# Opening of a transformer block on one core: one tile's statistics on ScalarE, scalings by halves, keys' exponentials later

## The chip, the cores and the metric

The kernel runs on one core of one Trainium2 chip. The metric is the device time of one execution in microseconds (us), from one launch. Five engines work beside each other, each through its own queue in order: TensorE (PE in the profile, with its weight loads as PEld), VectorE (DVE), ScalarE (ACT), GpSimd (POOL) and SyncE (SP), which here issues the DMAs. They wait for one another through semaphores.

## What is computed

The reference is a transformer block in fp32 with adaptive layer norms, over 2048 tokens of width 1024. Cut to what matters here:

```python
mod = silu(c) @ w_mod                       # six vectors of 1024
sa, ca, ga, sb, cb, gb = mod
h = layernorm(x) * (1 + ca) + sa            # over each token's 1024 values
x = x + ga * A(h)                           # attention with a memory, below
h = layernorm(x) * (1 + cb) + sb
x = x + gb * ((gelu(h @ w_gate) * (h @ w_up)) @ w_down)

def A(h):                                   # 32 heads of 32, 4 segments of 512 tokens
    for s in range(4):                      # qs, ks, vs: segment s of h @ wq, h @ wk, h @ wv
        a_dot = softmax(qs @ ks.T * scale + causal) @ vs
        a_mem = (phi(qs) @ M) / (phi(qs) @ z + 1e-6)
        o = g * a_mem + (1 - g) * a_dot     # g = sigmoid(beta)
        M += phi(ks).T @ vs ; z += phi(ks).sum()
    return concat(o) @ wo                   # phi(t) = t + 1 where t > 0, else exp(t)
```

The layer norm divides by the root of the variance plus 1e-5.

## The kernel before, in words

Activations are held transposed, as eight feature tiles of 128 features by 512 tokens for each segment. Matmuls get nearly fp32 accuracy from operands split in a high and a low part (`hi`, `lo`), and three products: high by high, low by high, high by low. The attention goes through 32 steps of four heads and one segment each; behind it come the output projection and the feed-forward part.

The change lies in the opening (`opening`, L1850), which prepares the first two segments and the first two steps. Every engine's order is written out by hand there: the string `OPENING` (L1845) is read word by word, each word emits some instructions, and each engine executes what it gets in that order.

For the second segment the words do the following.

- `x0` to `x3` load its four tiles of 128 tokens (`x1_load`, each 512 KB, named `rx` in the trace, L127). The loads go into four buffers that other raw data leave earlier.
- `t0` to `t3` take the statistics of a tile (`stats`, L1901): on VectorE two `bn_stats` of 512 columns (L227), their aggregate (L230), the variance plus eps (L232) and the negated mean (L1904); on POOL the power -0.5 (L233) and the product of mean and power (L1905).
- `b0` to `b3` normalize a tile in place (`scaled`, L1908), in two halves of 512 features: tile 0 on ScalarE (L1915), tiles 1 to 3 on VectorE (L1913).
- Each `N` is a piece of `norm_seg` (L332): the first makes the four transposes of feature tile 0 on PE (L341, tile `tpa`), and each later one reads a turned feature tile on ScalarE (`h`, L348), splits it in high and low parts (`hha`, L352 or L354; `hla`, L356 or L359), and transposes the next feature tile. Feature tiles 0 to 3 need the first halves of all four token tiles, 4 to 7 the second halves. Five `N` stand in the opening; the rest of them are called from the first step of the attention.
- Each `F` is a piece of `first_part` (L568) for the first segment: eight times the projections of one feature tile (L583, L586), then the keys' copies (`kn`, L415), then the values' copies (`vx`, L417), then the list `AFTER[0]`: `qo` splits the queries (`qh` L462, `ql` L466), `dq` copies them by DMA (L422), `kt` transposes the keys (L433) and splits them (`kh` L436, `kl` L437), `dk` copies them, `ek` takes the keys' exponentials (L444 on ScalarE, L445 and L447 on VectorE), and `ea` and `eb` do nothing in the first segment.
- `V` makes ten matmuls whose results nobody reads (L1944, `full`), which keep PE at work while it waits. `S` changes the pool of PSUM tiles. `g` works out the shares from beta on VectorE.

The projections of the second segment follow from the first attention step, by another `first_part`, again L583 and L586. Behind five of their eight feature tiles come the first scores (L615).

Of the kernel before, what the change touches and what calls it, by code (L numbers as in the profile page):

```python
# [13 lines left out]
AF = mybir.ActivationFunctionType  # L14
ALU = mybir.AluOpType
# [4 lines left out]
P = 128  # L20
D = 1024
KT = D // P
T = 2048
F = 3584
# [3 lines left out]
G = 8  # L28
# [4 lines left out]
EPS = 1e-5  # L33
# [3 lines left out]
def block_kernel(ctx: ExitStack, tc: tile.TileContext, x, c, wmod, wq, wkv, wo, beta, wg, wu, wd, out):  # L37
    nc = tc.nc
# [57 lines left out]
    def mm_ps(name):  # L96
        return psum.tile([P, L], F32, name=name, tag="mm", bufs=2)
# [12 lines left out]
    def o_ps(name):  # L110
        return psum.tile([P, L], F32, name=name, tag="o", bufs=1)
# [4 lines left out]
    def cs(shape, name, dt=F32, **kw):  # L116
        return const.tile(shape, dt, name=name, **kw)
# [48 lines left out]
    mhalf = cs([P, 4], "mhalf")  # L166
# [238 lines left out]
    def kv_tiles(n, nm):  # L405
        kn = t2("kn" + nm, "kn", shape=(P, 4, P))
        vx = t2("vx" + nm, "vx", bufs=3, shape=(P, 4, P + 2))
        nc.gpsimd.memset(vx[:, :, P:], 1.0)
        ST.setdefault(n, [None, ks_t[n % 2], None, None])[2] = vx
        return kn, vx  # L410

    def kv_out(ps, kn, vx, t, n, parts="kv"):
        psv = ps.rearrange("p (t m) -> p t m", m=2 * P)
        if "k" in parts:
            nc.scalar.activation(kn[:, t:t + n], psv[:, :, :P], AF.Copy)  # L415
        if "v" in parts:
            nc.vector.tensor_copy(vx[:, t:t + n, :P], psv[:, :, P:])  # L417
# [6 lines left out]
    def after_kv(u, n, s, nm, get):  # L424

        ks = ks_t[n % 2]
        tiles = {}

        def turned():
            kn = get()[0]  # L430
            ps = s_ps("kT" + nm)
            for t in range(4):
                nc.tensor.transpose(ps[:, t * P:(t + 1) * P], kn[:, t], ident)  # L433
            kh = tiles["h"] = t2("kh" + nm, "sp", bufs=4, dt=F32R)
            kl = tiles["l"] = t2("kl" + nm, "sp", bufs=4, dt=F32R)
            nc.scalar.activation(kh, ps, AF.Copy)  # L436
            nc.vector.tensor_sub(kl, ps, f32(kh))  # L437

        def expo():
            kn, vx = get()  # L440
            if s < NSEG - 1:
                knf = kn.rearrange("p a b -> p (a b)")
                e = tmp_tile("ek" + nm)
                nc.scalar.activation(e, knf, AF.Exp)  # L444
                nc.vector.tensor_scalar_min(e, e, 1.0)  # L445
                pk = t2("pk" + nm, "pk", shape=(P, 4, P))
                nc.vector.scalar_tensor_tensor(pk.rearrange("p a b -> p (a b)"), knf, 0.0, e, op0=ALU.max, op1=ALU.add)  # L447
                PK[n] = pk, vx

        u["kt"] = turned  # L450
        u["dk"] = lambda: spread(ks, ((0, tiles["h"]), (1, tiles["h"]), (2, tiles["l"])))
        u["ek"] = expo
# [115 lines left out]
    def first_part(n, g, s):  # L568

        nm = f"{g}_{s}"  # L570
        u = {}
        kn, vx = kv_tiles(n, nm)
        kv = [mm_ps(f"kv{nm}_{tp}") for tp in range(2)]
        psq = o_ps("q" + nm)
        after_kv(u, n, s, nm, lambda: (kn, vx))
        after_q(u, n, s, nm, lambda: psq)
        for kt in range(KT):
            hi, lo = hT[s][kt]
            wq_, wk_ = (W[g][i].rearrange("p h (k m) -> p h k m", m=m) for i, m in ((0, P), (1 + kt // 4, 2 * P)))
            for last in range(2):  # L580
                for a, b in (((0, hi), (1, hi)), ((0, lo),))[last]:
                    for t in range(4):
                        nc.tensor.matmul(kv[t // 2][:, 2 * P * (t % 2):2 * P * (t % 2 + 1)], b[:, t * P:(t + 1) * P],  # L583
                                         wk_[:, a, kt % 4], start=(kt == a == last == t % 2 == 0),
                                         stop=(kt == KT - 1 and last == 1), skip_group_check=True)
                    nc.tensor.matmul(psq, wq_[:, a, kt], b, start=(kt == a == last == 0),  # L586
                                     stop=(kt == KT - 1 and last == 1))
            yield
        for tp in range(2):
            kv_out(kv[tp], kn, vx, 2 * tp, 2, "kv" if s else "k")  # L590
        yield
        if s == 0:
            for tp in range(2):
                kv_out(kv[tp], kn, vx, 2 * tp, 2, "v")
            yield
        for q in AFTER[s].split():
            u[q]()
        yield

    def scores(u, n, g, s):  # L600
# [287 lines left out]
    def feed_forward():  # L888
# [950 lines left out]
    none = iter(())  # L1839
    proj = projections()  # L1840
    gab = []
    AFTER = ('qo kt ek dq ea dk eb', 'kt qo ea eb dk dq ek')
    HI_DVE = ((), (1, 5, 7))
    LO_DVE = ((), (0, 1, 5, 6, 7))
    OPENING = (  # L1845
# [3 lines left out]

    def opening():  # L1850
        x0 = [[], []]
        for i in range(4):
            for h in range(2):
                tag, bufs = ("pt0", 4) if h == 0 else ("sj", 3) if i < 3 else ("pq", 2)
                t = t2(f"x0_{i}_{h}", tag, bufs=bufs)
# [4 lines left out]
        spare = [f32(w[:, h]) for w in free for h in range(2)]  # L1860
        got, raw0, x1t, x1h = {}, {}, [], [[], []]
# [37 lines left out]
        sc = {}  # L1899

        def stats(s, i, halves):  # L1901
# [3 lines left out]
            nc.gpsimd.tensor_mul(mr, mr, rs)  # L1905
            sc[s, i] = rs, mr

        def scaled(s, i, hs, halves):  # L1908
            rs, mr = sc[s, i]
            for h in hs:  # L1910
                t = halves[h][i]
                if s and i:
                    nc.vector.tensor_scalar(t, t, rs, mr, op0=ALU.mult, op1=ALU.add)  # L1913
                else:
                    nc.scalar.activation(t, t, AF.Identity, bias=mr, scale=rs)  # L1915
# [5 lines left out]
        for u in OPENING.split():  # L1921
            n = int(u[1:]) if u[1:] else 0
            if u[0] == "p":
                pair(n)
            elif u[0] == "x":
                x1_load(n)
                for h in range(2):
                    x1h[h].append(x1t[n][:, h * L:(h + 1) * L])
            elif u[0] == "D":
                for k in range(4):  # L1930
                    nc.scalar.activation(dgs[n][:, k * P:(k + 1) * P], ident, AF.Identity,
                                         scale=scol[:, 4 * n + k:4 * n + k + 1])
            elif u[0] == "r":
                nc.tensor.matmul(scp[:, n * L:(n + 1) * L], ones, dgs[n], start=True, stop=True)
            elif u[0] == "e":
                nc.scalar.activation(scb[:, n * L:(n + 1) * L], scp[:, n * L:(n + 1) * L], AF.Copy)
            elif u[0] == "k":
                nc.scalar.activation(ks_t[n][96:128], selj[96:128].unsqueeze(2).to_broadcast([32, 4, L]), AF.Copy)
            elif u[0] == "W":
                for q in range(3):  # L1940
                    nc.tensor.matmul(s_ps(f"full0_{q}"), ones, dgs[0], start=True, stop=True)
            elif u[0] == "V":
                for q in range(10):
                    nc.tensor.matmul(s_ps(f"full1_{q}"), W[0][1][:, 0, :P], W[0][1][:, 0, :L], start=True, stop=True)  # L1944
            elif u[0] == "G":
                nc.scalar.activation(gall, bb, AF.Exp, scale=-1.0)
            elif u[0] == "g":
                shares()
            elif u[0] in "st":
                stats("st".index(u[0]), n, (x0, x1h)[u[0] == "t"])  # L1950
            elif u[0] == "a":
                scaled(0, n // 2, (n % 2,), x0)
            elif u[0] == "b":
                scaled(1, n, (0, 1), x1h)
            elif u[0] == "C":
                mod_col(*got[8 + n])
            elif u[0] == "c":
                mod_col(*got[n])
            elif u[0] == "K":
                nc.scalar.activation(W[0][1][:, 0], raw0[1], AF.Copy)  # L1960
            elif u[0] == "L":
                nc.vector.tensor_sub(W[0][1][:, 1], raw0[1], f32(W[0][1][:, 0]))
            elif u[0] in "qv":
                next(low["q.v".index(u[0])])
            elif u[0] == "n":
                next(nseg)
            elif u[0] == "N":
                if not nseg1:
                    nseg1.append(norm_seg(1, x1h))
                next(nseg1[0])  # L1970
            elif u[0] == "F":
                if not first:
                    first.append(first_part(0, 0, 0))
                next(first[0])
            elif u[0] == "S":
                s_all()
# [146 lines left out]
```

## Time and profile before

| | us |
|---|---|
| median of 3 runs | 2658.8 |
| lowest and highest of them | 2657.3, 2660.1 |
| the profiled execution | 2657.93 |
| its span, first to last instruction | 2656.2 |
| PE busy | 2629.0 |
| VectorE busy | 1749.7 |
| ScalarE busy | 1382.8 |
| POOL busy | 1062.1 |

A row of the timeline gives the start and the duration in us, the engine, the line of the kernel, the operation, the tile written and the tiles read, the shapes and how many instructions were merged in the row; a bracket at its end gives the idle time before it and who ended it. Rows of one engine may overlap a little, as its instructions are pipelined.

### The profile page before, as it was taken

The numbers are of one execution on the slowest core, as the hardware profiler recorded it, in microseconds if no ns is written. First come the engines' busy times: TensorE is split into PE (matmuls) and PEld (weight loads), VectorE is DVE, ScalarE is ACT, GpSimd is POOL, SyncE is SP. The second block draws the span as 40 slices with busy tenths as digits, with TensorE's granted clock in tenths as the row PEclk, the third lists the DMA queues.
The fourth block names the chain that finished last, engine by engine and source line by source line (L and its number), as shares of the span: only waits on it lengthen the run. The fifth ranks groups of instructions, "written<-read, shape, count | busy, mean of one in ns | idle before, by whom it ended". The sixth has DMA issues, their size and how long they took to land.

```text
span 2656.2 us, 42510 instructions
## 1 busy us (share of the span) xinstructions
PE 2629.0 (99%) x13889; PEld 2185.7 (82%) x13889; DVE 1749.7 (66%) x3688; ACT 1382.8 (52%) x3163; POOL 1062.1 (40%) x1598
## 2 busy tenths in 40 slices
PE   8999999999999999999999999999999999999999
PEld 6888888888888788888877888788888888888887
DVE  8677656767677745787876556667767554574456
ACT  6778767776777734566663434333333333243323
POOL 4333334433333533445567664687778100000000
PEclk9999999999999999999999999999999999999999
DMA  7455444534534558488989778899999886885563
GB/s 270 124 152 151 120 135 137 152 106 128 151 113 119 167 178 286 155 307 290 337 319 331 268 280 312 334 370 355 362 365 366 306 319 219 281 296 189 188 212 120
DMA packets 286591, 622.04 MB, mean 234 GB/s; under 512 B 29344, under 2 KB 53920, under 8 KB 286368
## 3 DMA queue, kind: packets, MB, share of 16 engines
q1 hardware_dynamic: 286368, 619.32, 69.0%
q8 instruction: 109, 1.79, 0.3%
q14 instruction: 114, 0.93, 0.1%
HBM read 380.65 MB, written 188.22 MB: 214 GB/s over the span
## 4 chain that ended last, share of the span: by engine, by line
PE 92%; DMA 3%; DVE 2%; ACT 2%; issue 1%; POOL 0%; SPq 0%; DVEq 0%; ACTq 0%; POOLq 0%
PE y L1702 20%; PE f L1501 17%; PE kv L397 9%; PE pb L1273 7%; PE y L781 6%; PE q L403 6%; PE pc L1273 5%; PE pa L1273 5%; PE S L615 3%; PE O L715 3%; PE T L703 3%; PE vT L518 2%; PE kT L518 1%; PE num L671 1%; PE M L654 1%; ACT sj L619 1%
## 5 line engine op out<-in xcount | busy, mean ns | idle before, releaser
L1702 PE MATMUL y<-B,L 128*128 128x512 f32 x2352 | 533.6, 389 | 0.0
L1702 PEld LDWEIGHTS y<-B,L 128*128 128x128 f32 x2352 | 441.4, 188 | 92.0 <-DVE L L931 0.4
L1501 PE MATMUL f<-A,B 128*128 128x512 f32 x2016 | 460.2, 390 | 3.2 <-DVE A L931 2.4
L1501 PEld LDWEIGHTS f<-A,B 128*128 128x128 f32 x2016 | 379.2, 188 | 84.1 <-DVE A L931 4.6
L619 ACT ACTIVATE sj<-sj,mm 128x384 f32<-128x384 f32 (+3 forms) x512 | 281.1, 552 | 41.8 <-DVE mm L617 41.3
L706 POOL TENSOR_SCALAR_AFFINE_SELECT pt<-pt 128x128 f32<-128x128 f32 x512 | 167.7, 350 | 330.2 <-ACT pt L705 322.2
L617 DVE CUSTOM_DVE_ANT_0 sj<-S,mask 128x384 f32<-128x384 f32 (+3 forms) x512 | 228.2, 488 | 96.8 <-PE S L615 70.1
L705 ACT ACTIVATE pt<-T 128x256 f32<-128x256 f32 (+3 forms) x512 | 182.3, 443 | 131.2 <-PE T L703 128.7
L1273 PE MATMUL pb<-AA,BB 128*128 128x512 f32 x1008 | 245.9, 391 | 4.5 <-DVE y L1296 2.9
L934 ACT ACTIVATE L<-X 128x512 fp32r<-128x512 f32 x168 | 105.8, 630 | 260.3 <-PE y L1702 171.6
L1273 PEld LDWEIGHTS pb<-AA,BB 128*128 128x128 f32 x1008 | 188.7, 188 | 46.1 <-DVE y L1296 3.4
L931 DVE TENSOR_TENSOR L<-X,L 128x512 fp32r<-128x512 f32 x168 | 115.8, 691 | 148.7 <-ACT L L934 148.6
L388 POOL TENSOR_TENSOR w<-r,w 128x256 fp32r<-128x256 f32 x180 | 134.0, 775 | 142.9 <-ACT w L382 142.9
L1528 ACT ACTIVATE g<-f 128x512 f32<-128x512 f32 x56 | 33.5, 598 | 288.4 <-PE f L1501 288.4
L397 PE MATMUL kv<-w,hha 128*128 128x256 f32 x896 | 174.4, 285 | 0.8 <-POOL w L388 0.8
L1273 PE MATMUL pc<-AA,BB 128*128 128x512 f32 x672 | 163.5, 391 | 0.2 <-DMA AA<-hl_d 0.2
L1273 PE MATMUL pa<-AA,BB 128*128 128x512 f32 x672 | 162.6, 390 | 0.0
L1273 PEld LDWEIGHTS pc<-AA,BB 128*128 128x128 f32 x672 | 126.8, 189 | 27.0 <-DMA AA<-hl_d 0.5
L1273 PEld LDWEIGHTS pa<-AA,BB 128*128 128x128 f32 x672 | 126.0, 188 | 26.6 <-issue 0.5
L397 PEld LDWEIGHTS kv<-w,hha 128*128 128x128 f32 x896 | 143.8, 191 | 2.7 <-POOL w L388 1.6
L931 DVE TENSOR_TENSOR BB<-t_a,BB 128x512 fp32r<-128x512 f32 x98 | 82.4, 841 | 91.0 <-ACT BB L934 90.9
L781 PE MATMUL y<-wo,hho 128*128 128x512 f32 x384 | 126.5, 395 | 0.0
(302 smaller groups left out, 5425.5 us busy)
## 6 DMA issues: line engine op xcount, KB each, us to landing
B<-wc_d SPq DMA_DIRECT2D x112, 512.0 KB, 3.4
cg<-st_d SPq DMA_DIRECT2D x168, 256.0 KB, 6.3
st_d<-x SPq DMA_DIRECT2D x112, 256.0 KB, 3.4
hid_d<-g SPq DMA_DIRECT2D x56, 512.0 KB, 6.2
wc_d<-T SPq DMA_DIRECT2D x56, 512.0 KB, 5.4
X<-hid_d SPq DMA_DIRECT2D x112, 256.0 KB, 5.0
st_d<-y SPq DMA_DIRECT2D x98, 256.0 KB, 3.7
wr<-gd_d SPq DMA_DIRECT2D x84, 256.0 KB, 4.1
```

Of the source, the lines that this page charges most:

```text
L388: nc.gpsimd.tensor_sub(w[:, 1, c], r[:, c], f32(w[:, 0, c]))
L397: nc.tensor.matmul(ps, b[:, sl], w[:, a], start=(kt == 0 and a == 0 and b is hi), stop=(kt == KT - 1 and a == 1), **kw)
L403: nc.tensor.matmul(ps, w[:, a], b, start=(kt == 0 and a == 0 and b is hi), stop=(kt == KT - 1 and a == 1), **kw)
L617: nc.vector.tensor_tensor_reduce(out=sj[:, :nv], in0=ps[:, :nv], in1=mask[:, L - nv:], scale=-1.0, scalar=3.4e38, op0=ALU.add, op1=ALU.min ...
L619: nc.scalar.activation(sj[:, :nv], sj[:, :nv], AF.Exp, bias=mm[:, j, i:i + 1], scale=-1.0, accum_out=ll[:, i, j:j + 1])
L705: nc.scalar.activation(pt, ps[:, nn - n:nn], AF.Exp)
L706: nc.gpsimd.affine_select(pt[:, :P], pt[:, :P], pattern=[[1, P]], compare_op=ALU.is_ge, fill=0.0, base=0, channel_multiplier=-1)
L781: nc.tensor.matmul(ps, b[:, i * P:(i + 1) * P], w[:, a, g % 2], start=(g == 0 and a == 0 and b is hi), stop=(g == G - 1 and a == 1))
L931: f(*xs)
L1273: nc.tensor.matmul(ps, w[:, a, at:at + P], A["a", i, r, k][b], start=(r in (1, 5) and k == a == b == 0), stop=(k == 1 and a == 1), skip_gr ...
L1501: nc.tensor.matmul(ps, B[fc, i][:, a, kt * P:(kt + 1) * P], A[p, i, kt][b], start=False, stop=(kt == 3 and a == 1), skip_group_check=True)
L1702: nc.tensor.matmul(banks[t], ops[k][:, y, t * P:(t + 1) * P], B[slots[k]][:, x], start=(i not in (2, 4, 3) and j == 0 and x == 0 and y == ...
```

## The change

It replaces the end of the string and the list behind it, and adds a way of taking statistics:

```diff
-    AFTER = ('qo kt ek dq ea dk eb', 'kt qo ea eb dk dq ek')
+    AFTER = ('qo dq | kt dk | ek', 'kt qo ea eb dk dq ek')
...
-        [...] C7 x3 c7 n F t0 t1 t2 t3 F b0 S b1 b2 "
-        "b3 F F V N N N N N g ")
+        [...] C7 x3 c7 n F t0 t2 t3 u1 F b0 S y0 F F "
+        "y1 F V N N N F N N g ")
...
+        def stats_act(s, i, t, junk):
+            sm, nm, vs, rs, mr = (cs([P, 1], f"{q}{s}_{i}") for q in ("sm", "nm", "vs", "rs", "mr"))
+            nc.scalar.activation(junk, t, AF.Copy, accum_out=sm)
+            nc.scalar.activation(nm, sm, AF.Copy, scale=-1.0 / D)
+            nc.scalar.activation(junk, t, AF.Square, bias=nm, accum_out=vs)
+            nc.vector.tensor_scalar(rs, vs, 1.0 / D, EPS, op0=ALU.mult, op1=ALU.add)
+            nc.gpsimd.tensor_tensor(rs, rs, mhalf[:, :1], op=ALU.pow)
+            nc.gpsimd.tensor_mul(mr, nm, rs)
+            sc[s, i] = rs, mr
...
-                for q in range(10):
+                for q in range(6):
                     nc.tensor.matmul(s_ps(f"full1_{q}"), W[0][1][:, 0, :P], W[0][1][:, 0, :L], start=True, stop=True)
...
+            elif u[0] == "u":
+                stats_act(1, n, x1t[n], spare[0])
+            elif u[0] == "y":
+                for i in (2, 3, 1):
+                    scaled(1, i, (n,), x1h)
```

In `first_part` a `|` in the list now ends a piece, so that the list takes three `F`. In words: the statistics of tile 1 are taken by ScalarE, as a sum, a mean, and a sum of squares about that mean, with VectorE left one small operation and POOL the same pair, which stands behind tile 3's pair. The scalings of tiles 2, 3 and 1 go by halves: the first halves of all three, then the values' copies and the split of the queries, then the second halves, then the split of the keys. The keys' exponentials move behind feature tile 1 of the second segment. The fills are six and no longer ten. The order on PE is otherwise the same, and so is SP's.

More of the change, by code (lines that the diff above doesn't have):

```diff
@@ L596, in first_part @@
         for q in AFTER[s].split():
-            u[q]()
+            if q == "|":
+                yield
+            else:
+                u[q]()
         yield
```

2 rows, old and new, of the table OPENING are left out of this document.

## The prediction

> **What bounds the kernel now.** I read the page first, then the opening engine by engine in the timeline from 26 to 64 us, and then the landings of the four loads that the second segment starts from.
>
> ```profile
> span 2656.2 us, 42510 instructions
> PE 2629.0 (99%) x13889; PEld 2185.7 (82%) x13889; DVE 1749.7 (66%) x3688; ACT 1382.8 (52%) x3163; POOL 1062.1 (40%) x1598
> PE 92%; DMA 3%; DVE 2%; ACT 2%; issue 1%; POOL 0%; SPq 0%; DVEq 0%; ACTq 0%; POOLq 0%
> ```
>
> PE is busy 99% of the span and carries 92% of the chain, so only time in which PE has no useful work can be won. All edits lie between 37 and 53 us. There PE runs as follows:
>
> ```profile
> 41.66 0.40 PE L586 MATMUL q<-hla,w 128*128 128x512 f32 x1
> 42.06 0.71 PE L433 MATMUL kT<-ident,kn 128*128 128x128 f32 x4
> 42.53 2.56 PE L1944 MATMUL full<-w 128*128 128x512 f32 x10
> 44.93 0.38 PE L341 MATMUL tpa<-ident,rx 128*128 128x128 f32 x2
> 45.73 0.33 PE L341 MATMUL tpa<-ident,rx 128*128 128x128 f32 x1 [0.42 <-DVE rx L1913]
> 46.64 2.08 PE L341 MATMUL tpa<-ident,rx 128*128 128x128 f32 x17 [0.58 <-DVE rx L1913]
> 49.17 0.66 PE L341 MATMUL tpa<-ident,rx 128*128 128x128 f32 x4 [0.45 <-ACT h L348]
> 49.58 0.72 PE L583 MATMUL kv<-w,hha 128*128 128x256 f32 x4
> 61.19 3.21 PE L615 MATMUL S<-ks,qs 96*128 96x128 f32 x12
> ```
>
> The first segment's projections end at 42.06. Ten fill matmuls (L1944), which compute nothing, follow the keys' transposes; then come the transposes of the normalized second segment (L341, four to a feature tile, here called turn 0, 1, ...). Turn 0 waits twice for a scaling on VectorE. Turns 1 to 4 run at once. Turn 5 waits for ScalarE's read of an earlier turn, since its bank must come free. At 49.58 the projections of the second segment begin, and from there PE works without a gap until the scores at 61.19. The whole change is therefore worth what it does to that start at 49.58; later work shifts with it, and PE's fill time counts nothing unless it ends last. 0.2% of the time, about what a measurement of this kernel can tell from no change, is 5.3 us, and the whole stretch from 42.06 to 49.58 is 7.5 us.
>
> **The statistics.** On VectorE and its helper POOL:
>
> ```profile
> 37.12 1.29 DVE L227 BATCH_NORM_STATS2 sta<-rx 128x6 f32<-128x512 f32 x2 [0.44 <-DMA rx<-x]
> 38.89 1.27 DVE L227 BATCH_NORM_STATS2 sta<-rx 128x6 f32<-128x512 f32 x2
> 40.65 1.28 DVE L227 BATCH_NORM_STATS2 sta<-rx 128x6 f32<-128x512 f32 x2
> 42.43 1.28 DVE L227 BATCH_NORM_STATS2 sta<-rx 128x6 f32<-128x512 f32 x2
> 44.09 0.15 DVE L232 TENSOR_SCALAR rsa<-mva 128x1 f32<-128x1 f32 x1
> 44.16 0.15 DVE L1904 TENSOR_SCALAR mr<-mva 128x1 f32<-128x1 f32 x1
> 44.22 2.82 DVE L1913 TENSOR_SCALAR rx<-rx,rsa,mr 128x512 f32<-128x512 f32 x6
> 46.95 0.75 DVE L417 COPY vx<-kv 128x256 f32<-128x256 f32 x2
> 47.62 0.68 DVE L466 SCALAR_TENSOR_TENSOR ql<-q,qh 128x512 fp32r<-128x512 f32 x1
> 48.22 0.68 DVE L437 TENSOR_TENSOR kl<-kT,kh 128x512 fp32r<-128x512 f32 x1
> 42.53 0.55 POOL L233 TENSOR_TENSOR rsa<-rsa,mhalf 128x1 f32<-128x1 f32 x1
> 44.32 0.93 POOL L233 TENSOR_TENSOR rsa<-rsa,mhalf 128x1 f32<-128x1 f32 x1 [0.97 <-DVE mr L1904]
> 45.33 0.39 POOL L1905 TENSOR_TENSOR mr<-mr,rsa 128x1 f32<-128x1 f32 x1
> ```
>
> One tile's statistics cost 1.77 us (38.89 less 37.12). Taking tile 1 off VectorE seems to bring tiles 2 and 3 forward by that much. But the data are not there. The issue of each load and its time to landing (min/median/max), for tiles 2 and 3 in turn:
>
> ```profile
> L127 SPq DMA_DIRECT2D rx<-x x1: 327/327/327, 36.4 to 36.4; - x1
> DMA to landing us min/median/max: 3.5/3.5/3.5
> L127 SPq DMA_DIRECT2D rx<-x x1: 328/328/328, 37.1 to 37.1; - x1
> DMA to landing us min/median/max: 4.7/4.7/4.7
> ```
>
> Tile 2 lands at 39.9 and tile 3 at 41.8; tile 1 is there by 38.89, when its statistics started without a wait. The issues are behind slots that other work frees, and the change moves none of that. So tile 2's statistics start at 39.9, not at 38.89, and tile 3's at about 41.83 in place of 42.43. Of 1.77 us saved, 0.60 is left.
>
> ScalarE's part, from these rows:
>
> ```profile
> 27.37 1.06 ACT L192 ACTIVATE w<-rv 128x1024 fp32r<-128x1024 f32 x1
> 34.09 0.21 ACT L1946 ACTIVATE gall<-bb 128x32 f32<-128x32 f32 x1
> 38.70 0.63 ACT L354 ACTIVATE hha<-h 128x512 fp32r<-128x512 f32 x1
> 41.62 0.66 ACT L415 ACTIVATE kn<-kv 128x256 f32<-128x256 f32 x2 [2.29 <-PE kv L583]
> 42.17 1.52 ACT L1915 ACTIVATE rx<-rx,mr,rsa 128x512 f32<-128x512 f32 x2
> 47.01 0.78 ACT L348 ACTIVATE h<-tpa,modT 128x512 f32<-128x512 f32 x1 [1.83 <-PE tpa L341]
> 62.10 0.19 ACT L619 ACTIVATION_READ_ACCUMULATOR sj<-sj,mm 128x1 f32 x1
> ```
>
> Copy of 1024 columns 1.06, its accumulator 0.19, the mean 0.21, Square 1.06 and again 0.19 make 2.7 us; the Square's bias operand adds 0.15 at most (h, with two operands per partition, takes 0.78, a plain copy 0.63), and overlap of neighbours takes about as much away. It starts behind the hha copy at 39.3 and ends near 41.9 (42.3 at the worst). The gap of 2.29 us ahead of kn covers all but 0.3 of it: kn starts near 41.9, the keys' transposes follow, and six fills at 0.24 (2.40 for ten, 42.53 to 44.93) end at 44.2. Nothing late comes of this, since turn 0 waits longer. VectorE's small operation on the variance (0.15) stands behind tile 3's statistics at 43.6, so its wait for ScalarE is already over; without that cover everything from the scalings on would wait behind it. Square does not occur in this stretch. If it brought a table load of some 1.3 us (two operations of 512 columns), and with kn at 43.2 the fills (2.3 us after kn as above) end at 45.5 and qh (0.55 for kn, 1.41 for the two scalings, 0.6 for itself) at 45.8, still ahead of turn 0 and of ql below: no cost.
>
> **The scalings.** Six operations take 2.73 us (44.22 to 46.95), 0.455 each. Before, turn 0 needed the fifth of them. Now it needs the third (tile 1's first half), but that one hangs on a POOL pair, power and product, which stands in POOL's queue behind tile 3's pair. Worked out: tile 3's rows move from 44.16, 44.22 and 44.32 by 0.60, and one tiny operation comes in between (0.07): tile 2's half starts at 43.69, tile 3's power at 43.72. A power costs 0.55 beside statistics and 0.93 where a scaling had just begun (44.32). Here a scaling has just begun too, so I take 0.93: to 44.65, product 44.73 to 44.92, tile 3's half at 44.98. Tile 1's power at 44.88 is ahead of that half, so 0.55: to 45.43, product 45.51 to 45.70, tile 1's half at 45.76 (45.38 if no power is stretched, 46.34 if the second power and product are stretched to 0.93 and 0.39 as well). It ends at 46.30. Three transposes remain where one remained; at 0.11 each ScalarE's h starts at 46.95 against 47.01. So the first half gains 0.06 us.
>
> The row of 0.93 bears on a rule. The Trainium skill, "SBUF — State Buffer", section "Who interferes with whom", says that VectorE in a two-port mode and GpSimd lock each other out of a shared port for a whole instruction, whoever issued first. The row agrees for POOL (44.32 plus the rest of a 0.455 scaling plus 0.55 is 45.2, recorded 45.25); but the six scalings run on at 0.455 beside it, so VectorE is not seen to wait. If VectorE did wait as the rule has it, tile 3's half would wait for tile 1's power and tile 1's product for that half, and the sum below would be about +0.9 instead of +0.15.
>
> **The second halves** now stand behind the values' copies (0.67, 46.95 to 47.62) and ql (0.60, 47.62 to 48.22): from tile 1's first half at 45.76, 0.455 later 46.21, then 46.88, and the three second halves from 47.48, the last starting at 48.39 and ending at 48.93. Turn 4 is the first that needs them. Before, they were done by 47.04 and turn 4 ran in the block of x17 that ended at 48.72. So a wait moves in: turn 4 at 48.99, its three last transposes 0.33, turn 5 0.41 (49.17 to 49.58), projections at 49.73. Turn 5's bank is free by then (49.17 less 0.06). **The step gives back what the first gained: 49.73 against 49.58, +0.15 us**, with -0.25 and +0.75 as the ends for the powers.
>
> **Edits with one answer.** kl stands behind the second halves and ends near 49.5; the first low part on VectorE follows by 50.2. PE wants it after two of the three groups of a feature tile's matmuls; five feature tiles and the eight transposes of turns 6 and 7 (0.9 us) fill 49.58 to 61.19, 2.1 us each, so that is 1.4 us in, at 51.1. The keys' exponential moves behind feature tile 1 on ScalarE (the next h is 0.6 us later, and feature tile 2 has 4 us until PE wants it) and on VectorE from ahead of kl's successors to behind them; its product is read only after the scores at 61.19. SP's queue keeps its order: the ks copies wait for kl, 0.7 us later than before and still 11 us ahead of the scores that read them, and the loads behind them are for the steps after. The shares of beta move by under a microsecond and are read behind the scores too. All of these: 0.
>
> **The sum.** The profiled execution took 2657.93 us, 0.9 under the median of the three runs (2658.8); on its scale 2658.1, on the median's 2659.0.
>
> **The rivals.**
> *Earlier data* (faster, 12%). Were tile 3 in place by 40.65, statistics would follow each other and everything above come 1.18 us sooner: projections at 48.55, -1.0, 2657.8 us. For it: DMA is nearly idle while that tile is outstanding.
>
> ```profile
> 40.00:41.00 1.00, 1.00 (x10) 0.96 (x9) 0.86 (x5) 0.00 (x0) 1.00 (x3) 1.00 0.55 209
> 41.00:42.00 1.00, 1.00 (x7) 0.69 (x6) 0.97 (x3) 0.38 (x2) 0.92 (x3) 1.00 0.04 16
> ```
>
> At a share of 0.04 only stragglers are left, and another execution may have none. Against it: the bulk itself ends at 41, which brings only the 0.16 until tile 2's statistics end at 41.67.
>
> *The clock* (slower, 8%). With four fills fewer and turn 0 later served, PE idles from about 44.4 to 46.3 in one piece.
>
> ```profile
> core 0: 2656.2 us, clock 0.998
> 28.00:31.40 3.40, 1.88 (x14) 1.55 (x13) 3.37 (x6) 3.03 (x5) 2.30 (x4) 1.00 1.02 407
> ```
>
> The stretch from 28.0 to 31.4 had PE busy for 1.88 of 3.40 us and kept clock 1.00; the new stretch from 44.3 to 47.7 would have about 1.5, and it decides if that is too little. All slow phases of the execution cost 0.002 of 2656.2, 5.3 us; one more is between nothing and that, say 2.7: 2661.7 us, slower, though inside the 0.2%. The Trainium skill, "TensorE: Matmul & The Clock Gate", section "Part 1", has the clock halved after an idle window of about 3.4 us; one window at half rate would lose 1.7 and give 2660.7, and by that rule a gap of 1.9 us is too short to bring it.
>
> That the change doesn't do what it says has no chance of its own: the forecast already is that the statistics taken off VectorE bring little, as a landing and POOL's pair end last.
>
> **How the numbers follow.** Forecast 74%, 2659.0, with the powers' ends 2658.6 to 2659.6; earlier data 12%; clock 8%; 6% for what I have not seen, to either side. The three runs lie -1.5 and +1.3 about their median, which I add outside: from the earlier data's 2657.8 down to 2656.6, and from 2659.6 up to 2661.2, which takes in most of the clock's lower half. Over 5.3 us in either direction needs something unseen or the top of the clock's range: faster 2%, slower 3%, within 95%.
>
> **What would show it.** Right: tile 3's statistics start at its landing near 41.8 with a wait for DMA ahead of them; ScalarE's Square ends near 42 and kn starts under 0.5 us later than 41.62; turn 0 waits in one piece of about 1.9 us for VectorE; turn 4 waits for a second half near 49; projections start within 49.3 to 50.3; clock 1.00 throughout. Wrong: statistics back to back from 38.89; kn at 43 or later; h ahead of 46.3; a clock under 1.00 between 44 and 62; or a start of the projections that moves while the time of the scores at 61.2 does not move with it.

## The result, and the profile after

| | before | after |
|---|---|---|
| median of 6 runs, us | 2659.0 | 2673.7 |
| lowest and highest | 2654.6, 2660.1 | 2672.8, 2674.9 |
| the profiled execution: span, us | 2656.2 | 2673.1 |

The ratio is 1.006, with an interval of 1.005 to 1.007: slower by 14.7 us. The predicted range ended at 2661.2. The chance given to slower by over 0.2% was 0.03.

The opening cannot hold 14.7 us. What counts there is the start of the second segment's projections, at 50.58 in place of 49.58 (PE's timeline of the changed kernel):

```profile
42.94 0.71 PE L433 MATMUL kT<-ident,kn 128*128 128x128 f32 x4
43.41 1.63 PE L1957 MATMUL full<-w 128*128 128x512 f32 x6
44.88 0.27 PE L341 MATMUL tpa<-ident,rx 128*128 128x128 f32 x1
47.21 1.97 PE L341 MATMUL tpa<-ident,rx 128*128 128x128 f32 x16 [2.06 <-DVE rx L1926]
49.84 0.98 PE L341 MATMUL tpa<-ident,rx 128*128 128x128 f32 x7 [0.66 <-DVE rx L1926]
50.58 0.72 PE L583 MATMUL kv<-w,hha 128*128 128x256 f32 x4
```

So 1.0 us of it arises here in these two executions, and 15.9 of the 16.9 us between the spans come later. The table of stages finds them. Its columns are the stretch, its length, the busy time and the number of instructions of PE, PEld, DVE, ACT and POOL, then the granted clock of PE, the share of DMA and its GB/s. Before:

```profile
2000.00:2100.00 100.00, 100.00 (x443) 82.84 (x442) 65.78 (x82) 35.19 (x66) 60.66 (x65) 1.00 0.93 339
2200.00:2300.00 100.00, 100.00 (x443) 82.81 (x442) 44.27 (x68) 27.57 (x45) 0.00 (x0) 1.00 0.70 236
```

After:

```profile
2000.00:2100.00 100.00, 100.00 (x443) 82.81 (x442) 67.83 (x83) 36.51 (x69) 61.65 (x66) 1.00 0.92 336
2200.00:2300.00 100.00, 100.00 (x430) 80.43 (x429) 44.74 (x69) 27.11 (x46) 0.00 (x0) 1.00 0.68 226
```

PE is busy for all of each stretch, at clock 1.00. Up to about 2120 us it does nearly as many matmuls as before; from there to the end it does 430 where it did 443. That is the down projection. "99% busy" hides it: a matmul that takes longer is as busy as before. The groups, with busy time and mean ns at the end, show it too. Before:

```profile
L1702 PE MATMUL y<-B,L 128*128 128x512 f32 x2352 | 533.6, 389 | 0.0
L1501 PE MATMUL f<-A,B 128*128 128x512 f32 x2016 | 460.2, 390 | 3.2 <-DVE A L931 2.4
```

After:

```profile
L1705 PE MATMUL y<-B,L 128*128 128x512 f32 x2352 | 549.0, 395 | 0.0
L1504 PE MATMUL f<-A,B 128*128 128x512 f32 x2016 | 460.4, 390 | 3.1 <-DVE A L934 2.4
```

The same 2352 matmuls cover 549.0 us and not 533.6: 233.4 ns for each in place of 226.9, 15.4 us in all. The gate and up projections (f) are as they were. Neither line's source changed.

### The profile page after: what moved, and what is told of

It reads as the page before. It is cut to its first block, busy times and chain, and to the rows that moved or that the text cites. A ratio compares the mean times of both kernels' runs of the same rounds, so it can differ in the third digit from the quotient of the medians.

```text
span 2673.1 us, 42500 instructions
## 1 busy us (share of the span) xinstructions
PE 2641.6 (99%) x13885; PEld 2183.6 (82%) x13885; DVE 1751.0 (66%) x3684; ACT 1385.1 (52%) x3168; POOL 1062.4 (40%) x1598
## 4 chain that ended last, share of the span: by engine, by line
PE 91%; DMA 4%; DVE 2%; ACT 1%; POOL 1%; issue 1%; SPq 0%; DVEq 0%; ACTq 0%; POOLq 0%
PE y L1705 21%; PE f L1504 17%; PE kv L397 9%; PE pb L1276 7%; PE y L784 6%; PE q L403 6%; PE pa L1276 5%; PE pc L1276 5%; PE S L618 3%; PE O L718 3%; PE T L706 3%; PE vT L518 2%; PE kT L518 1%; PE num L674 1%; PE M L657 1%
## 5 line engine op out<-in xcount | busy, mean ns | idle before, releaser
L1705 PE MATMUL y<-B,L 128*128 128x512 f32 x2352 | 549.0, 395 | 0.0
```

The costliest lines, as they stand in the source:

```text
L1705: nc.tensor.matmul(banks[t], ops[k][:, y, t * P:(t + 1) * P], B[slots[k]][:, x], start=(i not in (2, 4, 3) and j == 0 and x == 0 and y == ...
```

## The experiments

**What was suspected.** `cs(...)` without a tag makes a new buffer. The five small tiles of `stats_act` take 32 bytes per partition each, 160 in all, and the pools of the left side stand behind them. By the addresses that the built programs assign, L (the down projection's stationary operand) moves from 3456 to 3616, and so does all that stands behind it; B (its moving operand) is on the right side and stays at 180096. Theory 'place': it is this move. Rival 'phase': the later opening shifts transfers and other engines' work against PE.

First four kernels, on one chip. `p160` and `p192` are the kernel before with a wider constant tile and nothing else:

```diff
-    mhalf = cs([P, 4], "mhalf")
+    mhalf = cs([P, 44], "mhalf")     # p160; p192 has 52
```

> The kernel before, with one constant tile (mhalf) 160 bytes wider per partition and nothing else changed, so that all tiles of the left side stand where they stand in the changed kernel. Theory 'place' (the five small tiles of the new statistics push the operand tile L from a multiple of 64 bytes to 32 past one, and each of the 2352 matmuls of the down projection takes 6.6 ns longer): about 2659 + 15.6 = 2674 us, y<-B,L at 395 ns in the groups and 87 matmuls in 20 us. Rival 'phase' (the later opening moves transfers and other engines' work against PE for the rest of the execution): 2659 us, 389 ns, 90 in 20 us.

Measured 2674.2 us, before 2657.7 on that chip, ratio 1.006 (1.0045 to 1.0075).

```profile
L1702 PE MATMUL y<-B,L 128*128 128x512 f32 x2352 | 549.0, 395 | 0.0
```

The whole loss is there with the opening of before, to a tenth of a microsecond in the group. 'Phase' falls.

> The kernel before, with the same tile 192 bytes wider, so that L moves by a multiple of 64. Theory 'place' in the form that the offset within 64 bytes counts: 2659 us, 389 ns. Theory 'place' in the form that any move away from the first place costs (a distance between tiles, a bank): about 2674 us, 395 ns. Rival 'phase': 2659 us.

Measured 2663.8 us, 1.0021 (1.0012 to 1.003), which neither form expected.

```profile
L1702 PE MATMUL y<-B,L 128*128 128x512 f32 x2352 | 538.8, 391 | 0.3 <-DVE L L931 0.3
```

A multiple of 64 bytes is not enough, and yet it is less dear than 160.

`a32` is the changed kernel with `mhalf` 12 columns wide, so 192 bytes again:

> The changed kernel, with mhalf 32 bytes wider, so that the tiles of the left side stand 192 bytes and not 160 behind their first place, and L on a multiple of 64 again. Theory 'place': the down projection is back at 389 ns and the time at that of the kernel before plus what the opening alone costs, 2658.5 to 2661 us. Rival 'phase': still about 2674 us and 395 ns.

Measured 2662.6 us, 1.0019 (1.0009 to 1.0028).

```profile
L1705 PE MATMUL y<-B,L 128*128 128x512 f32 x2352 | 539.0, 391 | 0.3 <-DVE L L934 0.3
```

The group is that of `p192`, with another opening. 'Phase' fails again; 'place' is right, but its rule of 64 bytes is wrong.

`aedge` moves the other operand:

```diff
-    edge.tile([P, 24], F32, name="edge")
+    edge.tile([P, 16], F32, name="edge")
```

> The changed kernel, with the tile that spaces the right side 32 bytes narrower: B and all of the right side stand 32 past a multiple of 64, as L does. If it is L's own offset that costs: 395 ns for y<-B,L still, about 2674 us. If it is that L and B differ in their offset: 389 ns, about 2660 us. If each misplaced operand costs for itself: over 400 ns in the down projection and also more than 390 in f<-A,B and pb<-AA,BB, whose operands all move, 2690 us or more.

Measured 2672.3 us, 1.0054 (1.0039 to 1.0069).

```profile
L1705 PE MATMUL y<-B,L 128*128 128x512 f32 x2352 | 546.7, 395 | 0.0
L1504 PE MATMUL f<-A,B 128*128 128x512 f32 x2016 | 460.4, 390 | 3.1 <-DVE A L934 2.4 <-DVE cg L1521 0.6
```

The second form misses (it had 389 ns) and so does the third (it had 2690 us or more); the 395 ns and the time are what the first had, L's own offset. Against it stands f: both its operands are on the right side, 32 bytes off, and it does not slow, so an operand's own offset does not cost there. And y changed (546.7 from 549.0) as B alone moved. That pointed to the distance between L and B; `aedge112` below decides between the two.

**The distance.** In the kernel before, B less L is 180096 - 3456 = 176640, which is 345 times 512. The buffers of L and those of B lie 4096 bytes apart, and a matmul's parts begin in them at multiples of 512, so this holds for every pair. Four kernels more, on a second chip, where the kernel before took 2659.0 us. `a352` moves L on to 512 bytes (`mhalf` 96 columns), `aedge112` leaves L where the change put it and lowers B by 352 (`edge` 112 columns), `bedge` is the kernel before with `edge` at 16 columns, and `a0` moves nothing, since the small tiles use buffers that are there:

```diff
-            sm, nm, vs, rs, mr = (cs([P, 1], f"{q}{s}_{i}") for q in ("sm", "nm", "vs", "rs", "mr"))
+            st = cs([P, 2, 6], f"st{s}_{i}", tag="st", bufs=4)
+            sm, nm, vs = (st[:, 0, q:q + 1] for q in range(3))
+            rs, mr = (cs([P, 1], f"{q}{s}_{i}", tag=q, bufs=4) for q in ("rs", "mr"))
```

> The changed kernel with mhalf 352 bytes wider, so that L stands 512 bytes behind its first place. Theory 'distance' (what counts is where the stationary operand L stands against the moving operand B, modulo 512 bytes; in the kernel before the difference is a multiple of 512 in every matmul stage): 389 ns, 226.7 from matmul to matmul, 2656.5 to 2658.5 us. Rival 'absolute' (L's own address, or any move): 391 ns or more, 2662 us or more.

Measured 2657.6 us, 0.9997 (0.9988 to 1.0006).

```profile
L1705 PE MATMUL y<-B,L 128*128 128x512 f32 x2352 | 533.7, 389 | 0.3 <-DVE L L934 0.3
```

> The changed kernel with the spacing tile of the right side 352 bytes wider: B stands 352 bytes lower, L stays 160 higher than in the kernel before, so that both stand 32 past a multiple of 64 and their difference is again a multiple of 512. Theory 'distance': 389 ns in the down projection, 2656.5 to 2658.5 us. Rival 'offset within 64 bytes': 395 ns, 2670 us or more, and slower f<-A,B and pb<-AA,BB too.

Measured 2658.0 us, 0.9996 (0.9987 to 1.0005).

```profile
L1705 PE MATMUL y<-B,L 128*128 128x512 f32 x2352 | 533.7, 389 | 0.3 <-DVE L L934 0.3
```

> The kernel before with the spacing tile 32 bytes narrower and nothing else: B and the right side stand 32 bytes higher, L where it was. Theory 'distance': the down projection slows although neither L nor the opening was touched, 391 to 396 ns, 2662 to 2675 us, while f<-A,B and pb<-AA,BB, whose two operands move together, stay at 390. Rival 'L alone': 389 ns, 2657.7 us.

Measured 2673.9 us, 1.0057 (1.0043 to 1.007).

```profile
L1702 PE MATMUL y<-B,L 128*128 128x512 f32 x2352 | 549.0, 395 | 0.0
L1501 PE MATMUL f<-A,B 128*128 128x512 f32 x2016 | 460.4, 390 | 3.2 <-DVE A L931 2.6 <-DVE cg L1518 0.6
```

'Distance' holds in all three: fast with L moved, fast with both moved, slow with B alone moved and L in its place. Of the large groups of matmuls only the down projection has one operand on each side; f, pb and y<-wo take both from one side, so their distance is the same in all these kernels.

The edits move all tiles of a side, so one rival is left: a clash of PE's reads with other engines' work or with transfers on the moved tiles. The traces speak against it. From start to start, the 294 matmuls of the group beside which VectorE, ScalarE and GpSimd all stood idle took 226.7 ns before, and the 303 such matmuls after the change took 233.7. Where no DMA packet was under way either, it is 226.8 (36 of them) and 233.8 (37). The loss is there with nothing at work beside PE.

> The changed kernel with the five small tiles of the new statistics in buffers that are there already (the unused turn of the tiles for the other tiles' statistics), so that no tile moves; the whole opening is as changed. Theory 'place': down projection at 389 ns, and what is left is the opening alone. The prediction's sum for it was +0.15 us with ends of -0.25 and +0.75; the two pairs of equal placement so far gave -0.5 and -1.2 between medians. So 2656.5 to 2658.5 us beside 2657.7 of the kernel before. Rival 'the opening costs': over 2660.

Measured 2657.5 us (11 runs), before 2659.0, ratio 0.9998 (0.9989 to 1.0007; the medians themselves give 0.9995).

```profile
L1705 PE MATMUL y<-B,L 128*128 128x512 f32 x2352 | 533.4, 389 | 0.0
```

This is the change without its side effect: no difference that the measurement can tell.

**Modulo what?** Three kernels, with one run each: the kernel before with `mhalf` at 12, 20 and 68 columns (`p32`, `p64`, `p256`).

> The kernel before with mhalf 32 bytes wider: L 32 bytes behind its first place. Theory 'distance' (modulo 512): slow, 391 to 396 ns in y<-B,L; a single look, read by the groups and not by the time. If the distance counts only from 128 bytes on: 389 ns.

```profile
L1702 PE MATMUL y<-B,L 128*128 128x512 f32 x2352 | 549.0, 396 | 0.0
```

> The kernel before with mhalf 64 bytes wider. If the distance counts modulo 64, 389 ns in y<-B,L; if modulo 128 or more, 391 ns or more. The 192 bytes of an earlier run (391 ns) speak for the second.

```profile
L1702 PE MATMUL y<-B,L 128*128 128x512 f32 x2352 | 549.0, 395 | 0.0
```

> The kernel before with mhalf 256 bytes wider. If the distance counts modulo 256, 389 ns in y<-B,L; if modulo 512, 391 ns or more. 192 and 512 bytes so far leave 64, 128 with an offset, 256 and 512 open.

```profile
L1702 PE MATMUL y<-B,L 128*128 128x512 f32 x2352 | 533.3, 389 | 0.0
```

One run each: 2671.5, 2674.7 and 2655.5 us, before 2658.2. 256 bytes are free, so my 512 was twice the period. Distances that differ by 256 were compared only at 0, 256 and 512; that the others repeat too is assumed. By distance modulo 256, with the group's busy time over 2352:

| L moved against B, bytes | modulo 256 | ns a matmul | kernels |
|---|---|---|---|
| 0, 256, 512 | 0 | 226.7 to 226.9 | before, a0, p256, a352, aedge112 |
| 32, 64 | 32, 64 | 233.4 | p32, p64 |
| 128 (both also 32 off) | 128 | 232.4 | aedge |
| 160 | 160 | 233.4 | after, p160 |
| 192 | 192 | 229.1, 229.2 | p192, a32 |
| -32 | 224 | 233.4 | bedge |

**The opening's own limit.** `a0u` is `a0` with tile 1's POOL pair ahead of tile 3's (`t2 u1 t3`, halves in the order 2, 1, 3).

> The changed kernel without moved tiles, and with tile 1's pair on POOL put ahead of tile 3's: u1 stands ahead of t3, and the halves go in the order 2, 1, 3. In all runs of the changed opening so far the second segment's projections started 9.4 to 9.7 us behind the start of tile 2's statistics, with two waits of about 0.35 of VectorE for POOL in it. If the order of POOL's pairs is what the first halves hang on: one of the waits goes, and 8.5 us. If it is ScalarE's statistics: VectorE waits ahead of tile 3's statistics and it stays at 9.4 or more. The time itself should be about that of a0, within the measurement.

One run: 2657.7 us. From VectorE's timeline, with rows left out:

```profile
40.91 1.29 DVE L227 BATCH_NORM_STATS2 sta<-rx 128x6 f32<-128x512 f32 x2 [0.98 <-DMA rx<-x]
...
42.61 0.14 DVE L1907 TENSOR_SCALAR mr<-mva 128x1 f32<-128x1 f32 x1
42.88 0.15 DVE L1918 TENSOR_SCALAR rs<-st 128x1 f32<-128x1 f32 x1
42.95 1.28 DVE L227 BATCH_NORM_STATS2 sta<-rx 128x6 f32<-128x512 f32 x2
...
45.16 0.54 DVE L1928 TENSOR_SCALAR rx<-rx,rs,mr 128x512 f32<-128x512 f32 x1
46.04 0.55 DVE L1928 TENSOR_SCALAR rx<-rx,rsa,mr 128x512 f32<-128x512 f32 x1 [0.34 <-POOL mr L1908]
```

From ScalarE's and PE's:

```profile
42.59 0.18 ACT L1917 ACTIVATION_READ_ACCUMULATOR wm_a<-rx,st 128x1 f32 x1
...
49.79 0.72 PE L583 MATMUL kv<-w,hha 128*128 128x256 f32 x4
```

49.79 less 40.91 is 8.88: between the two theories. One of the two waits for POOL went, as expected; but the small operation on the variance (L1918) started 0.27 behind the one ahead of it, where 0.07 is usual, as ScalarE's sum was there only at 42.77 (42.59 and 0.18), and tile 3's statistics began 2.04 behind tile 2's and not 1.77. About 0.5 us was gained against the 9.37 of the changed kernel, far below what a time of the whole can show.

## Why the prediction was wrong

The step that failed is this sentence: "The whole change is therefore worth what it does to that start at 49.58; later work shifts with it". It took the change for a list of instructions. The change also allocates, and the allocation moved an operand of a stage 2000 us later, which put 15.4 us on the down projection. The same 15.4 us came with the old opening and moved tiles (`p160`), and none of it with the new opening and no moved tile (`a0`). No rival had it; it sat in the 6% for "what I have not seen, to either side". The prediction put the chance of slower at 3% because it looked for prices only in the stretch of 7.5 us from 42.06 to 49.58; a stage of 2352 matmuls, a fifth of the span, loses 0.2% of the execution with 2.3 ns for each (5.3 us over 2352).

Seen from behind, the signs were in the code and the trace: `cs` tiles without a tag in the diff, a spacing tile `edge` (L67 to L69) that no instruction reads, and one large stage whose operands come from two sides.

One sum of the prediction is off as well, without a part in this: 1.5 below 2657.8 and 1.3 above 2659.6 are 2656.3 and 2660.9, not 2656.6 and 2661.2.

The opening's steps, point by point, in rows picked from the changed kernel's timeline. VectorE:

```profile
38.66 1.29 DVE L227 BATCH_NORM_STATS2 sta<-rx 128x6 f32<-128x512 f32 x2 [1.21 <-DMA rx<-x]
41.21 1.29 DVE L227 BATCH_NORM_STATS2 sta<-rx 128x6 f32<-128x512 f32 x2 [0.70 <-DMA rx<-x]
42.98 1.28 DVE L227 BATCH_NORM_STATS2 sta<-rx 128x6 f32<-128x512 f32 x2
44.83 0.54 DVE L1926 TENSOR_SCALAR rx<-rx,rsa,mr 128x512 f32<-128x512 f32 x1
45.72 0.55 DVE L1926 TENSOR_SCALAR rx<-rx,rsa,mr 128x512 f32<-128x512 f32 x1 [0.35 <-POOL mr L1908]
46.61 0.55 DVE L1926 TENSOR_SCALAR rx<-rx,rs,mr 128x512 f32<-128x512 f32 x1 [0.34 <-POOL mr L1918]
```

- **Landings**: half right. Tile 2's statistics waited for their data (0.70), as forecast. Tile 3's, which were to wait too, did not: they followed 1.77 behind, and their load had landed by 42.5 (issued at 37.9, 4.6 to landing). So the gate is tile 2's landing and not tile 3's.
- **POOL's pair**: right as a limit, with two prices off. VectorE waited twice (0.35, 0.34), as the halves' starting times implied. But the power that I put at 0.93 took 0.55, and the second, at 0.55, took 0.67:

```profile
44.87 0.55 POOL L233 TENSOR_TENSOR rsa<-rsa,mhalf 128x1 f32<-128x1 f32 x1 [0.96 <-DVE mr L1907]
45.64 0.67 POOL L1917 TENSOR_TENSOR rs<-rs,mhalf 128x1 f32<-128x1 f32 x1
```

  The first began 0.04 behind a scaling and was not stretched. The row of 0.93 came with scalings back to back, and so did one in `a0u`, beside scalings that start at 44.70 and 45.16:

```profile
44.81 0.93 POOL L233 TENSOR_TENSOR rsa<-rsa,mhalf 128x1 f32<-128x1 f32 x1 [0.44 <-DVE mr L1907]
```

  By the rule of the exclusive port (the Trainium skill, "SBUF — State Buffer", "Who interferes with whom") a scaling in a two-port mode that began first holds GpSimd off until it ends. The two rows of 0.93 agree with it. The row of 0.55 fits only if the power reads near its end, and no row shows when it reads, nor in which mode the scalings ran. VectorE's scalings ran 0.54 and 0.55 beside the powers, so the rival in which VectorE waits for POOL's port did not come.
- **ScalarE**: right in the duration. The statistics took 39.98 to 42.63 (forecast 2.7 us), and kn followed at once. It started 0.91 later than before, where under 0.5 was forecast; 0.75 of that is the first segment's projections, whose last row starts at 42.41 and not at 41.66 in this execution:

```profile
39.98 1.04 ACT L1913 ACTIVATE wm_a<-rx 128x1024 f32<-128x1024 f32 x1
41.38 1.15 ACT L1915 ACTIVATE wm_a<-rx,nm 128x1024 f32<-128x1024 f32 x1
42.44 0.19 ACT L1915 ACTIVATION_READ_ACCUMULATOR wm_a<-rx,nm 128x1 f32 x1
42.53 0.64 ACT L415 ACTIVATE kn<-kv 128x256 f32<-128x256 f32 x2
```

- **Turn 0 and turn 4**: right. There is one wait of 2.06 us for turn 0 (forecast about 1.9), and a new one of 0.66 for the second halves at turn 4 (forecast 0.27, 48.99 less 48.72). The clock stayed at 1.00 over that gap, with PE busy for 1.34 of 3.40 us, so the clock's rival did not come:

```profile
44.30:47.70 3.40, 1.34 (x9) 0.90 (x8) 2.57 (x9) 1.24 (x3) 1.55 (x4) 1.00 0.41 118
```

- **The start of the projections**: near in size, wrong in what sets it. At 50.58 it lies outside the forecast 49.3 to 50.3, with the scores a microsecond later too (62.20 for 61.19). In seven profiled executions with the old opening it came 12.45 to 12.47 us behind the start of tile 0's statistics (49.58 less 37.12 in the kernel before), once 13.00. In six with the new one it came 9.36 or 9.37 behind tile 2's (50.58 less 41.21 here), once 9.65; the forecast had 9.83 (49.73 less 39.9). So the old opening hangs on the start of tile 0's statistics, which waited for the landing in six of the seven, and the new one on the landing of tile 2. Both starts move from one execution to the next, tile 0's between 37.12 and 38.60 in the old ones, tile 2's between 40.28 and 41.21 in the new. The means of the projections' start are 50.37 and 50.14 us: -0.2 where +0.15 was forecast, which that scatter cannot tell apart, so the agreement proves little. `a0` says of the whole time that the opening is worth nothing that can be measured.

## What to carry to other kernels

A change to a kernel is its instructions and its allocations: a new scratch tile, however small, can move every tile behind it, as five of 32 bytes did here. Put scratch into buffers that exist, or compare the addresses of the matmul operands of all stages before and after. When a time moves by more than the edited stretch holds, compare the count of matmuls in equal stretches first, since a busy share of 100% looks the same at 226.9 and at 233.4 ns.

## What the runs showed of the hardware

The time of a matmul here depends on where its stationary and moving operands stand in SBUF against each other, modulo 256 bytes: 226.7 to 226.9 ns at 0, 229.1 or 229.2 at 192, 232.4 to 233.4 at the other multiples of 32 that were tried (96 was not; 32, 64 and 256 have one run each). That holds for 128x512 matmuls of fp32r operands (f32 in the rows) that each have their own weight load; the shape was not varied. The Trainium skill, "TensorE: Matmul & The Clock Gate", "Part 2", says that loading the next weights does not steal read bandwidth from the running matmul. By that the distance would not matter; here it does, by up to 2.9%, and the measurement decides. That the weights' reads and the running matmul's hinder each other would explain it, but that is argued and not shown: the runs show that the distance decides, whatever the opening, the other engines and each operand's own offset are.
